# Chunked attention into a SoLU feed-forward: the attention's value products put directly behind the score products, and half of the attention's SBUF transfers issued by GpSimd

## Chip, core and metric

One NeuronCore of one Trainium2 chip. The metric is device microseconds of one execution, lower is better. Times are medians of several executions.

## What is computed

`q`, `k`, `v` are float32 of 8 batches x 8 heads x 576 tokens x 64. Attention runs inside chunks of 64 tokens; its output, 4608 tokens x 512, goes through a feed-forward with a softmax-gated unit and a layer norm. The reference, cut to that:

```
q_c, k_c, v_c = (t.reshape(B, H, nc, 64, D) for t in (q, k, v))
scores = matmul(q_c, k_c.T) / sqrt(D);  attn = softmax(scores)
x = matmul(attn, v_c)                       # -> (4608, 512)
h = x @ w_in                                # 512 -> 1024
solu = h * softmax(h)
ln = (solu - mean) / sqrt(var + 1e-06) * g_ln
out = ln @ w_out                            # 1024 -> 512
```

## The kernel before

The 4608 tokens are 36 tiles of 128 tokens (two chunks each). The large products are made in one-pass float32 form from high and low parts, so that each feed-forward product is three matmuls: `ffn_in` (tile `ph`, 24 matmuls of 128x512) takes `x_h`, `x_l` against `wi_h`, `wi_l`; `ffn_out` (tile `po`, 24 matmuls) takes `z_h`, `z_l` against `wo_h`, `wo_l`. The attention's two products are small: `scores` (`sx<-kT,qT`) and `values` (`sx<-attn_t,v_sb`), 8 matmuls of 64x128 each in the program, which the profile records as x16. Both write the one PSUM tile `sx` of two banks: bank 0 the scores, bank 1 the attention's output.

The first five tiles, the weights and the first loads are laid out by a hand-written list of words (`START`). From tile 5 on, one pass of the loop at the end works on several tiles at once. For tile i it: turns q and k of tile i+3 (`qk_turn`, VectorE transposes into `qT`, `kT`); turns `z` of tile i-1 (`z_turn`); splits `z` of the oldest queued tile into `z_h`, `z_l`; does `ffn_in(i)`, then `scores(i+3)`; starts `solu_a(i)`; and then runs three thirds of `ffn_out` of an older tile (`part()`, 8 matmuls each) with work between them: `softmax_a(i+3)`, `solu_b(i)`, `softmax_b(i+3)` and `values(i+1)` ahead of the second third, `attn_turn(i+3)` and `variance(i)` ahead of the last. `values` also copies its result out of PSUM as `x_h` (ScalarE) and `x_l` (VectorE). While `order.on` is set (from tile 5), TensorE, VectorE, ScalarE and GpSimd keep the order in which this is written. DMAs that are issued through `nc.sync` and `nc.gpsimd` are not held so: where they stand in their queues is left to the framework's scheduler.

Two operands change partitions by way of SBUF-to-SBUF DMAs, once for two tiles: VectorE transposes 32x32 blocks in place (`z` into `z_b`, `s_e` into `a_b`), and then 16 DMAs move the blocks of `z_b` to `z_t` (12 issued by SyncE, 4 by GpSimd), and 8 DMAs move those of `a_b` to `attn_t` (all issued by SyncE, L456). `attn_t` is a single buffer for a pair of tiles: `values` of the first tile of the pair waits for all 8 DMAs, and the next pair's DMAs wait for `values` of the second tile.

SyncE's queue (SP) also issues the loads: `q_st` and `k_st` (L293, 16 DMAs each for a batch, let out 14 to a tile) and `v_sb` (L352, one or two DMAs to a tile). GpSimd (POOL) does three vector operations per tile (`z<-z,nmean`, `s_e<-s_e,s_rinv`, `r<-u,mhalf`).

L42 is the helper through which the four ordered engines issue, so the profile shows most instructions at that line; they are told apart by tiles.

Of the kernel before, what the change touches and what calls it, by code (L numbers as in the profile page):

```python
# [27 lines left out]
class Order:  # L28
    """Engines whose instructions, while `on`, stay in the order they are written in."""

# [20 lines left out]
def chunk_attention_then_solu_ffn(  # L51
# [14 lines left out]
    P = 128  # L66
    CH = 64                      # tokens of an attention chunk
    NCH = S // CH                # chunks of a batch
    HP = H // 2                  # pairs of heads
    G = S // 32                  # groups of 32 tokens in a batch  # L70
    NT = B * S // P              # tiles of 128 tokens (two chunks)
    NCC = DM // P
# [46 lines left out]

    # ---- weights: to float32, then to high and low parts of 12 bits each (which is  # L120
    # exact), as products of one pass carry them. A piece is 128 rows of 512 columns.
    HALF = FF // 2
# [5 lines left out]
    def load_pair(x):  # L128
        """Two pieces by one load, in space that the tiles' loop takes over."""
        where, tag, bufs = (  # L130
            (work, "z_b", 1), (work, "z_t", 2), (stage, "q_st", 2), (stage, "k_st", 2)
        )[x if x < 2 else 2 + x % 2]
        raw = where.tile([P, 2, HALF, raw_words], U32, name="w_raw", tag=tag, bufs=bufs)
        src = (w_in, w_out)[x // NCC]
        m = x % NCC
        if x < NCC:
            dst, src = raw.rearrange("p x a b -> p (x a b)"), src[m * P:(m + 1) * P, :]
        else:
            dst = raw.rearrange("p x a b -> p x (a b)")
            src = src[2 * m * P:2 * (m + 1) * P, :].rearrange("(x p) n -> p x n", x=2)  # L140
        if x == 0:
            for n in range(2):
                cols = slice(n * HALF * raw_words, (n + 1) * HALF * raw_words)
                early[n:n] = [(dst[:, cols], src[:, cols])]
        else:
            nc.sync.dma_start(dst, src)
        for half in range(2):
            raws[pieces[2 * x + half]] = raw[:, half]
# [3 lines left out]
    def piece_scale(x):  # L152
        """The high words of a piece as float32 have the float64s' exponents in steps of 8;
        scaled by 2^-112 these have float32's bias (below float32's range they vanish,
        above it they are held at inf), and three bits to the left they are in place."""
        hi = raws[pieces[x]][:, :, 1]
        y = scaled[x] = work.tile(
            [P, HALF], F32, name="w_a", tag=("w_a", "o_sb")[x % 2]
        )
        act.activation(y, hi.bitcast(F32), AF.Abs, scale=2.0 ** -112)  # L160

    def piece_top(x):
        """A piece's float64s as sums of two float32: the high words' part, and the low
        words' with the same exponents. The high part of the weights is taken from the
        former."""
        kind, m, n = pieces[x]
# [52 lines left out]
    def piece_rest(x):  # L219
        """The sum of the two less the high part of the weights: their low part."""  # L220
        kind, m, n = pieces[x]
# [48 lines left out]

    # ---- attention operands: q as [(head of pair, d), pair, token]; k likewise by chunks,
    # with zeros where its head isn't the column's: [(head of pair, d), pair, chunk,
    # column's head of pair, key]; v as [(chunk, key), head, d]
    QT, V, QS, KS = {}, {}, {}, {}
    KT = [const.tile([P, HP, 2, 2, CH], F32, name=f"kT{x}") for x in range(2)]
    # the same for the attention, transposed: [(chunk, key), column's chunk, token / 32,
    # tile of pair, head, token % 32]
    AT = const.tile([P, 2, 2, 2, H, 32], F32, name="attn_t")
# [9 lines left out]
    def qk_loads(b):  # L288
        """The loads of a batch's q and k: [(head of pair, d / 32, token % 32), pair,
        token / 32, d % 32]."""  # L290
        def load(t, src, h, db):
            p0 = (h % 2) * D + db * 32
            nc.sync.dma_start(  # L293
                t[p0:p0 + 32, h // 2, :, :],
                src[b, h, :, db * 32:db * 32 + 32].rearrange("(g t) d -> t g d", t=32),
            )
        loads = []
        for src, dst, name in ((q, QS, "q_st"), (k, KS, "k_st")):
            t = stage.tile([P, HP, G, 32], F32, name=name)
            dst[b] = t  # L300
            loads += [
                (load, t, src, h, db) for h in range(H) for db in range(2)
            ]
        return loads
# [5 lines left out]
    def qk_turn(i):  # L310
        """A tile's q and k from their stage, transposed."""
        (b0, n0), (b1, n1) = chunk_of(i, 0), chunk_of(i, 1)
# [20 lines left out]
    def tile_parts(i):  # L333
        """A tile's parts of different batches: partitions, batch, first token."""
        (b0, n0), (b1, n1) = chunk_of(i, 0), chunk_of(i, 1)
        if b0 == b1:
            return [(0, P, b0, n0 * CH)]
        return [(0, CH, b0, n0 * CH), (CH, P, b1, n1 * CH)]

    def load_natural(i):  # L340
        """The first tiles' q and k, with tokens on partitions."""
        for x, src in enumerate((q, k)):
            for p0, p1, b, s in tile_parts(i):
                nc.sync.dma_start(
                    nat[p0:p1, i % 2, x],
                    src[b, :, s:s + p1 - p0, :].rearrange("h t d -> t h d"),
                )
# [28 lines left out]

    # ---- the stages of a tile of 128 tokens
    st = {}
    # a bank for the scores, one for the attention's output
    sx = ps_a.tile([P, 2, 512], F32, name="sx")  # L380
# [38 lines left out]
    def attn_transpose(i):  # L419
        """By the tensor engine, for the first tiles."""  # L420
        a = st.pop((i, "e"))
# [17 lines left out]

    # For the others 32 by 32 blocks are transposed in place, then the blocks change  # L440
    # quadrants, for two tiles at once
    def attn_turn(i):
# [8 lines left out]
        if i % 2 == 1:  # L451
            for c in range(2):
                for x in range(2):
                    for y in range(2):
                        to, of = c * CH + x * 32, c * CH + y * 32
                        nc.sync.dma_start(  # L456
                            AT[to:to + 32, c, y].rearrange("p s h t -> p (s h t)"),
                            ab[of:of + 32, x].rearrange("p s h t -> p (s h t)"),
                        )

    def values(i):
        for hp in range(HP):
            for j in range(2):
# [5 lines left out]
                    stop=True,  # L469
                )  # L470
        xv = sx[:, 1, :]
        xh = work.tile([P, NCC, P], F32R, name="x_h")
# [9 lines left out]
    def ffn_in(i):  # L482
        xh, xl = st[i, "x"]
        ph = st[i, "h"] = ps_h.tile([P, 2, HALF], F32, name="ph")
        # the first tile's by pieces of weights
        sums = [(n, cc) for n in range(2) for cc in range(NCC)]
# [21 lines left out]
    def solu_b(i):  # L508
# [10 lines left out]
        )  # L519
        # 1e-6 of the variance, in units of the unnormalised solu  # L520
        ssum = small.tile([P, 1], F32, name="ssum")
# [24 lines left out]

    # z with the feed-forward's features on partitions: 32 by 32 blocks are transposed in
    # place, then the blocks change quadrants, for two tiles at once
    turned = {}
# [34 lines left out]
    def z_transpose(i, f):  # L584
        """The same by the tensor engine, for the first and the last tiles."""
        z, _ = st[i, "n"]
# [9 lines left out]
    def ffn_out(i, part, parts):  # L596
        zh, zl = ZH, ZL
        # the last tile's by halves of the columns, of which one is stored ahead
        halves = 2 if i == NT - 1 else 1
# [32 lines left out]

    # ---- start: the first tiles by way of the tensor engine, weights behind them
    NAT = -(-S // P)             # tiles with the first batch's tokens

# [19 lines left out]

    # thirds of second products in the slots
    def direct(m):
# [17 lines left out]
    def third_ahead():  # L675
        """The same, with the halves of the next tile's operand where they find room."""
        m, p = queue.pop(0)
# [24 lines left out]
    for i in range(first, NT):  # L702
        order.on = i >= ORD
        # the loads of the batch after the one whose tiles come up
        if i + 3 < NT and next_batch < B and chunk_of(i + 3, 0)[0] == next_batch - 1:
# [9 lines left out]
        load_some(14)  # L715
        ffn_in(i)
        if i + 3 < NT:
            scores(i + 3)
        solu_a(i)

# [12 lines left out]
        if i + 1 < NT:  # L733
            values(i + 1)
        part()
# [38 lines left out]
```

## Time and profile before

| | |
|---|---|
| time, median of 3 executions | 543.99 us (543.41 to 545.03) |
| span of the profiled execution | 542.3 us |
| the median less that span | 1.7 us |
| mean granted TensorE clock | 0.994 |
| busy: PE / VectorE / ScalarE / GpSimd | 95% / 78% / 44% / 32% |
| matmuls per tile in the loop | 24 `ph`, 24 `po`, 16 + 16 recorded on `sx` |

The page does not give the profiled execution's own time apart from its span; the three timed executions lie 1.1 to 2.7 us above that span. A row of the timeline reads: start in us, duration in us, engine, line, operation, tile written <- tiles read, shape, how many; in brackets the idle time of the engine before it and what ended it. SPq and POOL rows with DMA_DIRECT2D are issues of DMAs: their duration is the issuing engine's time, and the landing of the data is told apart. Matmuls are pipelined: a 128x512 matmul is shown as 0.39 us long, but the next starts 0.23 us after it.

### The profile page before, as it was taken

The numbers are of one execution on the slowest core, as the hardware profiler recorded it, in microseconds if no ns is written. First come the engines' busy times: TensorE is split into PE (matmuls) and PEld (weight loads), VectorE is DVE, ScalarE is ACT, GpSimd is POOL, SyncE is SP. The second block draws the span as 40 slices with busy tenths as digits, with TensorE's granted clock in tenths as the row PEclk, the third lists the DMA queues.
The fourth block names the chain that finished last, engine by engine and source line by source line (L and its number), as shares of the span: only waits on it lengthen the run. The fifth ranks groups of instructions, "written<-read, shape, count | busy, mean of one in ns | idle before, by whom it ended". The sixth has DMA issues, their size and how long they took to land.

```text
span 542.3 us, 8909 instructions
## 1 busy us (share of the span) xinstructions
PE 515.1 (95%) x3038; PEld 403.0 (74%) x3038; DVE 425.4 (78%) x748; ACT 239.3 (44%) x386; POOL 174.7 (32%) x226
## 2 busy tenths in 40 slices
PE   2768899999999999999999999999999999999997
PEld 2445677777777777777777777777777777778886
DVE  4999998888888888888887888888878888875441
ACT  4848774544444333333333344433343343434342
POOL 6564742323232323232323232323132323232210
PEclk9998989999999999999999999999999999999999
DMA  8997794458663577657863776566753424142311
GB/s 237 348 230 154 120 156 77 113 126 161 136 147 98 126 148 147 144 130 140 147 148 103 144 160 138 138 136 148 147 134 79 121 75 123 53 107 78 102 45 59
DMA packets 206493, 72.18 MB, mean 133 GB/s; under 512 B 188592, under 2 KB 189232, under 8 KB 206064
## 3 DMA queue, kind: packets, MB, share of 16 engines
q1 hardware_dynamic: 198944, 57.85, 51.6%
q10 hardware_dynamic: 5328, 9.44, 4.9%
q0 software_dynamic: 2176, 4.33, 3.4%
q8 instruction: 24, 0.39, 0.3%
q14 instruction: 21, 0.17, 0.1%
HBM read 36.97 MB, written 9.44 MB: 86 GB/s over the span
## 4 chain that ended last, share of the span: by engine, by line
PE 80%; DVE 8%; SPq 7%; DMA 3%; ACT 1%; issue 1%; POOL 0%; DVEq 0%; POOLq 0%
PE po L42 36%; PE ph L42 31%; PE sx L42 11%; DVE w_a L42 4%; SPq L293 3%; SPq L456 2%; PE tp L42 2%; SPq L566 2%; DMA v_sb<-in_v_dram 1%; DMA w_raw<-in_moe_w_in_dram 1%; DVE w_p L42 1%; SPq L352 1%; DVE z L42 0%; ACT kT L42 0%; DVE s_sum L42 0%
## 5 line engine op out<-in xcount | busy, mean ns | idle before, releaser
L42 PE MATMUL po<-wo_l,z_h 128*128 128x512 f32 (+1 forms) x288 | 115.4, 401 | 0.0
L42 PE MATMUL po<-wo_h,z_l 128*128 128x512 f32 (+1 forms) x288 | 114.7, 398 | 0.0
L42 PE MATMUL ph<-wi_h,x_l 128*128 128x512 f32 x288 | 112.2, 390 | 2.5 <-DVE x_l L42 2.5
L42 POOL TENSOR_SCALAR z<-z,nmean 128x1024 f32<-128x1024 f32 x36 | 42.0, 1167 | 225.0 <-DVE ssum L42 204.0
L42 PE MATMUL ph<-wi_l,x_h 128*128 128x512 f32 x288 | 112.7, 391 | 0.3 <-ACT x_h L42 0.3
L42 PE MATMUL ph<-wi_h,x_h 128*128 128x512 f32 x288 | 112.1, 389 | 0.0
L42 PE MATMUL po<-wo_h,z_h 128*128 128x512 f32 (+1 forms) x288 | 111.7, 388 | 0.0
L42 ACT ACTIVATE z<-ph,h_nmax 128x1024 f32<-128x1024 f32 x36 | 40.3, 1119 | 140.6 <-DVE h_nmax L42 140.6
L42 DVE TENSOR_REDUCE h_nmax<-ph 128x1 f32<-128x1024 f32 x36 | 44.0, 1223 | 48.2 <-PE ph L42 48.2
L42 PEld LDWEIGHTS po<-wo_h,z_l 128*128 128x128 f32 x288 | 54.1, 188 | 15.7 <-issue 5.1
L42 PEld LDWEIGHTS ph<-wi_h,x_l 128*128 128x128 f32 x288 | 54.1, 188 | 14.3 <-DVE x_l L42 3.1
L42 PEld LDWEIGHTS po<-wo_l,z_h 128*128 128x128 f32 x288 | 54.1, 188 | 14.1 <-issue 5.1
L42 PEld LDWEIGHTS ph<-wi_l,x_h 128*128 128x128 f32 x288 | 54.1, 188 | 12.2 <-ACT x_h L42 0.7
L42 PEld LDWEIGHTS ph<-wi_h,x_h 128*128 128x128 f32 x288 | 54.1, 188 | 10.9
L42 PEld LDWEIGHTS po<-wo_h,z_h 128*128 128x128 f32 x288 | 54.2, 188 | 10.0
L566 POOL DMA_DIRECT2D z_t<-z_b x68 | 35.0, 520 | 45.4 <-DVE z_b L42 27.5
L42 DVE SCALAR_TENSOR_TENSOR z<-ph,z 128x1024 f32<-128x1024 f32 x36 | 44.1, 1224 | 6.2 <-ACT z L42 6.2
L42 ACT ACTIVATE sq<-z 128x1024 bf16<-128x1024 f32 x36 | 38.1, 1058 | 23.4 <-POOL z L42 23.4
L42 ACT ACTIVATE o_sb<-po,r 128x512 f32<-128x512 f32 (+1 forms) x36 | 24.6, 684 | 47.9 <-PE po L42 47.8
L42 DVE TENSOR_TENSOR z_l<-z_t,z_h 128x1024 fp32r<-128x1024 f32 (+1 forms) x35 | 39.6, 1131 | 6.8 <-ACT z_h L42 6.7
L42 ACT CAST z_h<-z_t 128x1024 fp32r<-128x1024 f32 (+1 forms) x35 | 35.0, 1001 | 22.0 <-ACT o_sb L42 7.4
L42 POOL TENSOR_TENSOR s_e<-s_e,s_rinv 128x512 f32<-128x512 f32 x36 | 37.8, 1049 | 20.7 <-DVE s_rinv L42 20.7
(91 smaller groups left out, 724.0 us busy)
## 6 DMA issues: line engine op xcount, KB each, us to landing
z_t<-z_b SPq DMA_DIRECT2D x192, 64.0 KB, 2.0
out_dram<-o_sb ACTq DMA_DIRECT2D x35, 256.0 KB, 2.7
v_sb<-in_v_dram SPq DMA_DIRECT2D x32, 256.0 KB, 3.5
q_st<-in_q_dram SPq DMA_DIRECT2D x112, 72.0 KB, 2.6
k_st<-in_k_dram SPq DMA_DIRECT2D x112, 72.0 KB, 3.3
attn_t<-a_b SPq DMA_DIRECT2D x120, 64.0 KB, 2.1
w_raw<-in_moe_w_out_dram SPq DMA_DIRECT2D x4, 1024.0 KB, 6.8
z_t<-z_b POOLq DMA_DIRECT2D x64, 64.0 KB, 2.8
```

Of the source, the lines that this page charges most:

```text
L42: ins = make(*args, **kwargs)
L293: nc.sync.dma_start(t[p0:p0 + 32, h // 2, :, :], src[b, h, :, db * 32:db * 32 + 32].rearrange("(g t) d -> t g d", t=32),)
L352: nc.sync.dma_start(V[i][p0:p1], v[b, :, s:s + p1 - p0, :].rearrange("h t d -> t h d"))
L456: nc.sync.dma_start(AT[to:to + 32, c, y].rearrange("p s h t -> p (s h t)"), ab[of:of + 32, x].rearrange("p s h t -> p (s h t)"),)
L566: (nc.gpsimd if x == y else nc.sync).dma_start(zt[x * 32:(x + 1) * 32, y, of].rearrange("p s a t -> p (s a t)"), zb[y * 32:(y + 1) * 32, x ...
```

## The change

Three edits. In the loop, `values(i + 1)` moves from ahead of the second third of `ffn_out` to directly behind `scores(i + 3)`, so that TensorE does both attention products in one stretch. The copies of its result out of PSUM, `x_h` and `x_l`, become a function of their own, `x_split`, and stay where they were. And of the 8 DMAs from `a_b` to `attn_t`, the four with x == y are issued by GpSimd. (Comments are taken out too, which shifts line numbers: what was L566 is L570.) The diff, cut to these:

```diff
                 for x in range(2):
                     for y in range(2):
                         to, of = c * CH + x * 32, c * CH + y * 32
-                        nc.sync.dma_start(
+                        (nc.gpsimd if x == y else nc.sync).dma_start(
                             AT[to:to + 32, c, y].rearrange("p s h t -> p (s h t)"),
                             ab[of:of + 32, x].rearrange("p s h t -> p (s h t)"),
                         )
...
     def values(i):
...
+        if not order.on:
+            x_split(i)
+
+    def x_split(i):
         xv = sx[:, 1, :]
...
         ffn_in(i)
+
         if i + 3 < NT:
             scores(i + 3)
+        if i + 1 < NT:
+            values(i + 1)
         solu_a(i)
...
         if i + 3 < NT:
             softmax_b(i + 3)
         if i + 1 < NT:
-            values(i + 1)
+            x_split(i + 1)
         part()
```

TensorE's order around one tile of the loop, before: the last matmul of `ffn_in`, the scores, a third of `ffn_out`, the values (a row without xN is one matmul).

```order
L42 MATMUL ph<-wi_h,x_l 128x512
L42 MATMUL sx<-kT_96,qT 64x128 x8
L42 MATMUL po<-wo_l,z_h 128x512
L42 MATMUL po<-wo_h,z_h 128x512
L42 MATMUL po<-wo_h,z_l 128x512
L42 MATMUL po<-wo_l,z_h 128x512
L42 MATMUL po<-wo_h,z_h 128x512
L42 MATMUL po<-wo_h,z_l 128x512
L42 MATMUL po<-wo_l,z_h 128x512
L42 MATMUL po<-wo_h,z_h 128x512
L42 MATMUL sx<-attn_t,v_sb 64x128 x8
L42 MATMUL po<-wo_h,z_l 128x512
```

The same place after the change:

```order
L42 MATMUL ph<-wi_h,x_h 128x512
L42 MATMUL ph<-wi_h,x_l 128x512
L42 MATMUL sx<-kT_96,qT 64x128 x8
L42 MATMUL sx<-attn_t,v_sb 64x128 x8
L42 MATMUL po<-wo_l,z_h 128x512
L42 MATMUL po<-wo_h,z_h 128x512
```

The values have moved ahead of eight `po` matmuls; this is so in each of the 28 tiles of the loop that have both products (i from 5 to 32).

SyncE's queue from one pair's transfers to `attn_t` to the next pair's, at a place where a batch's q and k are being loaded, before:

```order
L456 DMA attn_t<-a_b 32x512 x8
L293 DMA q_st<-in_q_dram 32x18x32 x14
L352 DMA v_sb<-in_v_dram 128x8x64
L293 DMA q_st<-in_q_dram 32x18x32 x2
L293 DMA k_st<-in_k_dram 32x18x32 x4
L566 DMA z_t<-z_b 32x512 x12
L293 DMA k_st<-in_k_dram 32x18x32 x4
L456 DMA attn_t<-a_b 32x512 x8
```

And after, the same stretch:

```order
L456 DMA attn_t<-a_b 32x512 x4
L293 DMA q_st<-in_q_dram 32x18x32 x14
L352 DMA v_sb<-in_v_dram 128x8x64
L293 DMA q_st<-in_q_dram 32x18x32 x2
L293 DMA k_st<-in_k_dram 32x18x32 x9
L570 DMA z_t<-z_b 32x512 x12
L293 DMA k_st<-in_k_dram 32x18x32 x3
L352 DMA v_sb<-in_v_dram 128x8x64
L456 DMA attn_t<-a_b 32x512 x4
```

Four `attn_t` issues have left the stretch, and the scheduler has put four more `k_st` and one more `v_sb` into it: 46 issues from the first `attn_t` of one pair to the first of the next, where 45 stood. This row pattern comes three times in the changed queue; before, two of the three held 45 issues and the first 42.

GpSimd's queue after the change, over two tiles:

```order
L42 TENSOR_TENSOR s_e<-s_e,s_rinv 128x512
L456 DMA attn_t<-a_b 32x512 x4
L42 TENSOR_TENSOR r<-u,mhalf 128x1
L42 TENSOR_SCALAR z<-z,nmean 128x1024
L42 TENSOR_TENSOR s_e<-s_e,s_rinv 128x512
L42 TENSOR_TENSOR r<-u,mhalf 128x1
L570 DMA z_t<-z_b 32x512 x4
```

The four new issues stand between `s_e` and `r` of every second tile; before, `r` followed `s_e` there. VectorE's and ScalarE's orders are the same before and after.

## The prediction

> **What bounds the kernel now.** First the page: how full TensorE is, and whether its clock was cut.
>
> ```profile
> span 542.3 us, 8909 instructions
> PE 515.1 (95%) x3038; PEld 403.0 (74%) x3038; DVE 425.4 (78%) x748; ACT 239.3 (44%) x386; POOL 174.7 (32%) x226
> core 0: 542.3 us, clock 0.994
> ```
>
> TensorE is busy 95% at full clock, and a busy TensorE may still lose time between groups, so next the chain of waits, over two tiles in the middle:
>
> ```profile
> 263.37 1.02 PE sx L42 x16
> ...
> 266.43 1.02 PE sx L42 x16
> ...
> 271.30 5.44 PE ph L42 x24
> 276.74 1.02 PE sx L42 x16
> ...
> 279.80 0.25 issue
> 280.05 1.09 PE sx L42 x16
> ...
> 290.46 1.02 PE sx L42 x16
> ```
>
> The chain is TensorE alone. A tile takes 276.74 - 263.37 = 13.37 us from scores to scores; the next takes 13.72, because its values started late. 24 `ph` in 5.44 us make 0.227 us per large matmul, so the 48 large ones take 10.88 us, and the two attention stretches cost (13.37 - 10.88)/2 = 1.24 us each. How much of that is work, and how much is going in and out? The timeline of one stretch, and of the one place in the start where values follow scores directly, with the time of a single small matmul:
>
> ```profile
> 303.45 0.39 PE L42 MATMUL ph<-wi_h,x_l 128*128 128x512 f32 x1
> 303.76 1.09 PE L42 MATMUL sx<-kT,qT 128*64 128x128 f32 x16
> 304.79 0.50 PE L42 MATMUL po<-wo_l,z_h 128*128 128x512 f32 x1
> 305.13 0.40 PE L42 MATMUL po<-wo_h,z_h 128*128 128x512 f32 x1
> ...
> 93.29 1.09 PE L42 MATMUL sx<-kT,qT 128*64 128x128 f32 x16
> 94.22 1.04 PE L42 MATMUL sx<-attn_t,v_sb 128*64 128x128 f32 x16
> L42 PE MATMUL sx<-attn_t,v_sb x464: 272/273/323, 132.6 to 506.4; 128*64 128x128 f32 x155
> ```
>
> Going in, the scores start 0.31 us after the last `ph` (0.227 is usual); going out, the first `po` holds the array 0.34 us instead of 0.227. In the start's place the values come 0.93 us after the scores began, with nothing lost between. The 1.04 us of those values less one matmul's 0.27 is 0.77 us for seven steps (the sixteen records run in pairs): 0.11 a step, 0.87 us for eight. So a stretch is 0.87 us of work and 1.24 - 0.87 = 0.37 us of going in and out.
>
> **Part 1: one stretch instead of two.** The second stretch loses its 0.37 us: 28 tiles x 0.37 = **10.4 us saved**. The lower bound of a tile's saving is 1.24 - 0.93 = 0.31 (8.7 us in all), if the values paid the start's 0.93.
>
> The values also stop waiting for what they waited for before. The view of the tile `sx` and one row of the timeline:
>
> ```profile
>   DVE s_e L42: 9.5, 26
> 387.73 1.09 PE L42 MATMUL sx<-attn_t,v_sb 128*64 128x128 f32 x16 [0.59 <-DMA attn_t<-a_b]
> ```
>
> Twice in the loop the values start late, for `attn_t` that has not landed: 0.35 us (13.72 - 13.37), with 0.25 of it in the chain, and here about 0.6. If these vanish they give **1.0 us**; whether they do is part 3.
>
> **Part 2: what VectorE pays.** The values' start is released by VectorE's `s_e`, which reads the other bank: waits go by the whole tile `sx`. With the values ahead of the softmax, its first step `s_nmax` will then wait for the values' end, not the scores'.
>
> ```profile
> 301.60 1.18 DVE L42 TENSOR_TENSOR z_l<-z_t,z_h 128x1024 fp32r<-128x1024 f32 x1
> 303.87 1.23 DVE L42 TENSOR_REDUCE h_nmax<-ph 128x1 f32<-128x1024 f32 x1 [1.09 <-PE ph L42]
> 305.01 0.68 DVE L42 TENSOR_REDUCE s_nmax<-sx 128x8 f32<-128x512 f32 x1
> 309.28 0.64 DVE L42 TENSOR_TENSOR x_l<-sx,x_h 128x512 fp32r<-128x512 f32 x1
> 310.62 0.71 DVE L42 STREAM_TRANSPOSE a_b<-s_e 128x512 f32<-128x512 f32 x1 [0.70 <-POOL s_e L42]
> ```
>
> Values would end at 303.76 + 0.93 + 1.04 = 305.73, so `s_nmax` and all behind it on VectorE slip by about 0.75 us. I cost this at nothing, and name the cover. `x_l` would end at 309.92 + 0.75 = 310.7; the next `ffn_in` starts 271.30 - 263.37 = 7.9 us after the scores, less the 0.37 saved, at 311.3, and needs `x_l` in its third matmul, at 311.8. VectorE then idles 1.1 us before `h_nmax`, for `ph`, in this tile (one with a batch boundary, more transposes than most); the slip of 0.75 and a tile shorter by 0.37 use up just that. Where it is gone, `h_nmax` starts later, under a `s_nmax` that waits anyway. On GpSimd, `r` stands behind four DMA issues of 0.5 us; it is used when its tile is stored, three tiles later.
>
> What is not free: `a_b` ends at 312.1 instead of 311.3 while the values that read it come sooner. New scores of the next tile: 303.76 + 13.0 = 316.8, values 317.7. From `a_b` to the values 5.6 us are left. Before, the next values came 3.06 us behind their scores (266.43 - 263.37), at 303.76 + 13.37 + 3.06 = 320.2, 8.9 us after `a_b`.
>
> **Part 3: whether `attn_t` lands in 5.6 us.** The rows of SyncE's queue at the ends of the three stretches of the order in which a batch is loaded, a row for each kind, and the landing times of `attn_t`, then of GpSimd's `z_t`:
>
> ```profile
> 111.38 4.96 SPq L456 DMA_DIRECT2D attn_t<-a_b  x8
> 137.52 5.50 SPq L456 DMA_DIRECT2D attn_t<-a_b  x8
> ...
> 297.99 4.99 SPq L456 DMA_DIRECT2D attn_t<-a_b  x8
> 311.41 0.44 SPq L352 DMA_DIRECT2D v_sb<-in_v_dram  x1
> 323.78 2.23 SPq L293 DMA_DIRECT2D k_st<-in_k_dram  x4
> 326.12 4.95 SPq L456 DMA_DIRECT2D attn_t<-a_b  x8
> ...
> 351.48 5.26 SPq L456 DMA_DIRECT2D attn_t<-a_b  x8
> 381.24 4.95 SPq L456 DMA_DIRECT2D attn_t<-a_b  x8
> DMA to landing us min/median/max: 1.9/2.1/4.4
> L566 POOL DMA_DIRECT2D z_t<-z_b x68: 496/497/715, 100.8 to 514.3; - x68
> DMA to landing us min/median/max: 1.7/2.7/4.2
> ```
>
> An issue costs SyncE about 0.62 us (4.95/8). In an ordinary pair its four last issues start 3 x 0.62 = 1.9 us after `a_b` and land 2.1 later: 4.0 us of the 5.6. GpSimd's four: 3 x 0.5 + 2.7 = 4.2, at worst 5.7. Both fit.
>
> In the loaded stretches SyncE is late by itself: 26.14, 28.13 and 29.76 us from pair to pair, where two tiles take 26.74. Before, 8 issues needed 7 x 0.62 + 2.1 = 6.4 of 8.9, so 2.5 us of lateness were free; the last was late by 3.0, and its values waited about 0.6. The rule holds there. After: the second and third swap four `attn_t` (0.62) for four `k_st` (2.23/4 = 0.56) and one `v_sb` (0.44): +0.2, 28.3 and 30.0. The first, 42 issues to 46, gets seven `k_st` and a `v_sb` for four `attn_t`: +1.9, 28.0. Two tiles now take 26.0, so SyncE is late by 2.0, 2.3 and 4.0, and only 5.6 - 4.0 = 1.6 us are free: waits of 0.4, 0.7 and 2.4. The 13.72 us tile shows a wait of 0.3 beyond the rule, which I add once: **3.8 us of new waits**. Bounds: none, if SyncE gains speed when half the transfers leave it; and with the third's pace (29.76/45 = 0.66 an issue) in all three, 46 x 0.66 - 26.0 - 1.6 = 2.8 each, 8.3.
>
> The Trainium skill, DMA: Bandwidth & Descriptors, section "Issuing engines are not separate DMA queues", says that issuing from more engines saves only the sequencer's time, "usually small relative to the DMA itself". By it SyncE's issues could not make the values late, and the sum would be the first rival's 532.6. Here the row decides: 0.62 us of issue against 2.1 of landing, and the issues of one queue add up.
>
> **The sum.** 542.3 - 10.4 - 1.0 + 3.8 = 534.7 us of span. The median of the runs lies 1.7 above the profiled span: **536.4 us**.
>
> **Rivals.**
> - *SyncE keeps up*: no new waits, 544.0 - 11.4 = 532.6. For it: each pair has four issues fewer. Against: at the three loaded places the scheduler filled the gap. 0.17.
> - *Waiting costs queue time*: the values of the first tile of a pair wait on eight semaphores, now right between small matmuls. If that eats these tiles' saving, 14 x 0.37 = 5.2: 541.6. Against: before, both tiles of a pair take 13.37. 0.05.
> - *SyncE late in more pairs*: the 8.3 us and 3 us in further pairs eat the gain, about 544. 0.08.
> - *GpSimd's half lands late, slower*. Its four issues stand beside VectorE's transposes, which follow `a_b`. Were they held until `z_b` is turned, 2.1 us of `qT`, `kT` and 1.25 of `z_b` (rows below) put the landing at 3.3 + 4.2 = 7.5 us, 1.9 past the 5.6, in 14 pairs: 26.6 us, 559.2. From a hold of 2.2 us it outweighs what the change saves (0.8 x 14 = 11). Against: GpSimd's `z_t` issues at 314.87 ran at 0.5 each beside VectorE's `z_l`. 0.09.
>
> ```profile
> 311.29 0.70 DVE L42 STREAM_TRANSPOSE qT<-q_st 128x512 f32<-128x512 f32 x1
> 311.92 1.38 DVE L42 STREAM_TRANSPOSE kT<-k_st 64x512 f32<-64x512 f32 x2
> 313.33 1.25 DVE L42 STREAM_TRANSPOSE z_b<-z 128x1024 f32<-128x1024 f32 x1
> 314.50 1.18 DVE L42 TENSOR_TENSOR z_l<-z_t,z_h 128x1024 fp32r<-128x1024 f32 x1
> 314.87 2.05 POOL L566 DMA_DIRECT2D z_t<-z_b  x4 [2.88 <-DMA q_st<-in_q_dram]
> ```
>
> The Trainium skill, SBUF — State Buffer, section "SBUF: two separate sides", states this hold for VectorE's two-port modes: GpSimd cannot write descriptors meanwhile, 620 ns becoming about 3100; by that figure four issues would take 12.4 us (an estimate), and the time would be far above 559. The `z_t` row shows none for `z_l`; no row shows GpSimd issuing beside a transpose.
>
> **How the numbers follow.** The forecast has 0.61. A measurement of this kernel can tell about 0.3%, 1.6 us, from no change. Faster: 0.61 + 0.17 + 0.05, **0.83**; same, the late-in-more-pairs case, **0.08**; slower **0.09**. The range leaves out only the slow rival and the worst of the waits: from no waits, 532.6 less 0.6 for the run's spread (543.41 against 543.99), **532.0**, to 8.3 us of waits, 540.9, and the semaphore rival's 541.6: **541.7**.
>
> **What would show it.** Right: TensorE's chain with one `sx` group of 32 per tile and 13.0 us from scores to scores in tiles without a wait; VectorE idle about 0.7 us before `s_nmax`, for TensorE's `sx`; the values waiting for `attn_t` from SyncE in about three loaded tiles, 3 to 4 us in all. Wrong: tiles at 13.37 (the stretch had no price of entry, or the semaphores took it); waits for GpSimd's DMAs in every pair; `ph` waiting for `x_l`.

## The result, and the profile after

| | before | after |
|---|---|---|
| median | 544.51 us (543.41 to 545.42, 4 executions) | 551.28 us (550.25 to 552.27, 4 executions) |
| span of the profiled execution | 542.3 us | 550.5 us |

The changed kernel takes 1.0118 of the time of before (95% interval 1.0096 to 1.0141): 1.2% slower, where 536.4 us was forecast and the range ended at 541.7.

The page first. The columns are as before.

```profile
span 550.5 us, 8913 instructions
PE 509.4 (93%) x3038; PEld 407.5 (74%) x3038; DVE 427.0 (78%) x748; ACT 235.6 (43%) x386; POOL 205.4 (37%) x286
```

TensorE is busy 5.7 us less than before, so one stretch does cost less than two; but the span is 8.2 us longer, so TensorE now stands idle some 14 us more. The chain of waits, over one tile near the end of the loop, where no batch is loaded any more:

```profile
408.16 1.90 PE sx L42 x32
...
421.16 1.90 PE sx L42 x32
```

One group of 32 on `sx`, and 421.16 - 408.16 = 13.00 us from scores to scores. Here the forecast's tile is exactly what came out. What TensorE waits for in the loop (110 to 530 us; total, times, longest):

```profile
PE sx L42 <- DMA attn_t<-a_b: 13.6, 10, 4.0
PE sx L42 <- DMA q_st<-in_q_dram: 0.6, 1, 0.6
```

Ten waits of 13.6 us in all, not three of 3.8. The busy time by stretch, for three tiles with a wait, from a tile's first `ph` to the next tile's (the columns after the length: busy time and count of PE, PEld, VectorE, ScalarE and GpSimd; granted clock; DMA share; GB/s):

```profile
247.94:262.11 14.17, 13.25 (x82) 10.67 (x81) 10.94 (x19) 5.20 (x8) 4.79 (x8) 1.00 0.90 167
329.06:344.64 15.58, 13.22 (x81) 10.67 (x80) 10.94 (x19) 5.20 (x8) 4.76 (x8) 1.00 0.65 132
383.77:402.57 18.80, 14.80 (x82) 11.84 (x81) 12.33 (x23) 5.20 (x8) 5.36 (x9) 0.91 0.55 118
```

The first is an ordinary pair (1.17 us over 13.00), the second and third are loaded stretches (2.58 and 5.80 over). In the third, TensorE is also busy 1.6 us longer for the same work, and its clock is 0.91; that is looked at in the last section. Over all tiles, the time above 13.00 adds up to 18.6 us: 13.6 and 0.6 of waits, 1.6 of slow clock, about 0.2 more at each wait (2.58 where the wait's row says 2.36), and some 0.5 left over. Of it 11.0 lies in the three loaded stretches (2.6, 2.6, 5.8) and 7.6 in the other tiles.

The balance of the spans: -10.4 for the stretch, -1.0 for the old waits, +18.6, and +0.9 because the loop began that much later: +8.1, against 550.5 - 542.3 = 8.2.

Now an ordinary pair (not one of the three loaded ones), from the end of `a_b` to the values, in the timeline (VectorE, ScalarE's queue, SyncE's queue, GpSimd, TensorE):

```profile
248.06 0.71 DVE L42 STREAM_TRANSPOSE a_b<-s_e 128x512 f32<-128x512 f32 x1 [0.70 <-POOL s_e L42]
248.86 0.34 ACTq L635 DMA_DIRECT2D out_dram<-o_sb  x1
249.12 3.29 SPq L456 DMA_DIRECT2D attn_t<-a_b  x4
249.33 2.01 POOL L456 DMA_DIRECT2D attn_t<-a_b  x4 [1.30 <-issue]
249.36 1.38 DVE L42 STREAM_TRANSPOSE kT<-k_st 64x512 f32<-64x512 f32 x2
255.48 1.09 PE L42 MATMUL sx<-attn_t,v_sb 128*64 128x128 f32 x16 [0.92 <-DMA attn_t<-a_b]
```

and the view of the tile `attn_t`, of this pair: SyncE's four issues (minimum, median and maximum in ns, first and last start) and the landing of all eight transfers:

```profile
L456 SPq DMA_DIRECT2D attn_t<-a_b x4: 513/589/1467, 249.1 to 251.8; - x4
DMA to landing us min/median/max: 3.5/4.5/4.8
```

`a_b` ends at 248.77. Forecast was a last issue 1.9 us later, at 250.7, landing by 252.8. The last issue of SyncE starts at 251.8, because SyncE came 0.35 us late and one of the four took 1.47 us, and no transfer lands in less than 3.5: nothing before 255.3, and the values start at 255.48. Beside them runs the output store of 256 KB that ScalarE issues 0.1 us after `a_b`. Over the whole kernel the same view gives:

```profile
L456 SPq DMA_DIRECT2D attn_t<-a_b x60: 507/588/1596, 112.3 to 496.5; - x60
L456 POOL DMA_DIRECT2D attn_t<-a_b x60: 496/496/581, 112.8 to 496.7; - x60
DMA to landing us min/median/max: 2.1/3.6/4.9
```

3.6 us where before showed 2.1, for both halves (SyncE's 3.7, GpSimd's 3.5), and in every pair the last transfer to land is one of SyncE's. The pair shown is among the worst. In the pair whose `a_b` ends at 222.34, SyncE starts 0.03 us later and its last issue is at 224.2, as forecast; the landing of its eight is

```profile
DMA to landing us min/median/max: 3.5/3.8/4.0
```

so that the last lands 5.75 us after `a_b`, and the values wait 0.5 us. And a loaded stretch, SyncE's queue at the third of them:

```profile
358.49 3.43 SPq L456 DMA_DIRECT2D attn_t<-a_b  x4
362.02 7.62 SPq L293 DMA_DIRECT2D q_st<-in_q_dram  x14
...
377.72 8.69 SPq L570 DMA_DIRECT2D z_t<-z_b  x12
...
389.71 2.74 SPq L456 DMA_DIRECT2D attn_t<-a_b  x4
```

GpSimd's four of this pair went out at 385.15, right behind `a_b`; SyncE's start at 389.71, 5.1 us after `a_b`, because the loads and the twelve `z_t` stand ahead of them. (In the other two loaded stretches they start 2.4 and 2.45 us after it. In four of the other pairs, too, SyncE is late, by 0.35 to 1.2 us.)

VectorE's group of `s_nmax`, the step that was to slip:

```profile
L42 DVE TENSOR_REDUCE s_nmax<-sx 128x8 f32<-128x512 f32 x36 | 24.8, 690 | 33.7 <-PE sx L42 33.7
```

It waits 33.7 us for `sx`, about 0.7 a tile and more where the values are late; `ph` waits for VectorE's `x_l` nowhere in the loop.

### The profile page after: what moved, and what is told of

It is laid out like the page before. It is cut to its first block, busy times and chain, and to the rows that moved or that the text cites. A ratio compares the mean times of both kernels' runs of the same rounds, so it can differ in the third digit from the quotient of the medians.

```text
span 550.5 us, 8913 instructions
## 1 busy us (share of the span) xinstructions
PE 509.4 (93%) x3038; PEld 407.5 (74%) x3038; DVE 427.0 (78%) x748; ACT 235.6 (43%) x386; POOL 205.4 (37%) x286
## 5 line engine op out<-in xcount | busy, mean ns | idle before, releaser
L42 PE MATMUL po<-wo_h,z_l 128*128 128x512 f32 (+1 forms) x288 | 112.1, 389 | 0.0
L570 POOL DMA_DIRECT2D z_t<-z_b x68 | 35.0, 520 | 45.3 <-DVE z_b L42 24.6
L42 PE MATMUL sx<-attn_t,v_sb 128*64 128x128 f32 x576 | 38.5, 275 | 14.2 <-DMA attn_t<-a_b 13.6
L42 DVE TENSOR_REDUCE s_nmax<-sx 128x8 f32<-128x512 f32 x36 | 24.8, 690 | 33.7 <-PE sx L42 33.7
L42 PEld LDWEIGHTS sx<-attn_t,v_sb 128*64 128x64 f32 x576 | 32.0, 137 | 19.4 <-issue 17.6
```

The source lines that it names most:

```text
L42: ins = make(*args, **kwargs)
L570: (nc.gpsimd if x == y else nc.sync).dma_start(zt[x * 32:(x + 1) * 32, y, of].rearrange("p s a t -> p (s a t)"), zb[y * 32:(y + 1) * 32, x ...
```

## Experiments

Four theories stood open. **Two queues**: eight transfers from two queues within 2 us, beside the store, take longer each. **SyncE's order**: loads ahead of `attn_t` make SyncE late. **False wait**: the slip of VectorE takes the 0.7 us that would have been enough. **GpSimd harms**: the half on GpSimd is the mistake itself. Each ratio is against runs of the kernel before on the same chip (medians 544.09, 543.51 and 544.15 in the three groups). They agree within 1 us with the 544.51 of the result, so times of different groups are compared directly below.

**e1: all eight transfers on SyncE again**, the values still moved.

```diff
-                        (nc.gpsimd if x == y else nc.sync).dma_start(
+                        nc.sync.dma_start(
```

> The changed kernel with all eight attn_t transfers back on SyncE; the values stay behind the scores. Theory (the eight transfers, close together and beside the output's store, land 3.5 to 3.7 us after their issue instead of 2.1, so GpSimd's half saves less than its issue time, but it does save): SyncE's eight need 7 x 0.62 + 2.1 = 6.4 us of the 5.6 there are, so the ordinary pairs wait about 1 us each, the three loaded ones 3 to 6; attn_t lands in 2.1 to 2.6 at the median; 550 to 556 us. Rival (GpSimd's queue is what made the transfers late): waits shrink and the time falls below 546.

573.62 us, 1.0535 (1.0508 to 1.0562). A pair's issues in the timeline of SyncE's queue, then the waits of TensorE, then the page's row of transfers (count, KB, median us to landing):

```profile
432.02 5.18 SPq L456 DMA_DIRECT2D attn_t<-a_b  x8
```

```profile
PE sx L42 <- DMA attn_t<-a_b: 27.8, 15, 4.0
```

```profile
attn_t<-a_b SPq DMA_DIRECT2D x120, 64.0 KB, 2.0
```

Landing is back at 2.0, so the longer landing does come with the second queue. But the last issue starts 4.6 us after the first in this pair, and the waits double. The half on GpSimd is worth 22 us here: *GpSimd harms* falls. The time is beyond the 550 to 556 expected: SyncE is also 1.1 to 1.9 us late in three further pairs, and behind five of the waits TensorE's clock falls (0.976 in the mean), which by the tiles' lengths costs some 9 us more.

**e2: the half on GpSimd alone**, values where they were before.

```diff
-                        nc.sync.dma_start(
+                        (nc.gpsimd if x == y else nc.sync).dma_start(
```

> The kernel before with half of the attn_t transfers issued by GpSimd and the values where they were. Theory (crowding by two queues at once): attn_t lands in 3.0 to 3.6 us at the median although the values have not moved; TensorE has 8.9 us, so nothing waits in ordinary pairs; 542.5 to 545 us. Rival (the transfers land late because everything behind the scores slipped by 0.75 us into the store and the loads): attn_t lands in 2.1 to 2.4. If GpSimd's queue harmed VectorE or the other transfers by itself, the time would be over 548.

545.17 us, 1.0012 (0.9997 to 1.0027): no difference. The view of `attn_t`, then TensorE's waits in the loop, all of them:

```profile
DMA to landing us min/median/max: 1.9/3.6/5.4
```

```profile
PE sx L42 <- issue: 0.4, 1, 0.4
```

The landing is as long as after the change, 3.6, and nobody waits for it, since 8.9 us are free there (one wait of 0.4 us is left, where SyncE is 3.0 us late). So the price was there, and only the move of the values made it due.

**e3: two PSUM tiles in place of `sx`**, so that `s_nmax` waits for the scores alone.

```diff
-    sx = ps_a.tile([P, 2, 512], F32, name="sx")
+    sx = ps_a.tile([P, 512], F32, name="sx")
+    ax = ps_a.tile([P, 512], F32, name="ax")
...
```

> The changed kernel with the PSUM tile sx made into two tiles of one bank, so that the softmax no longer waits for the values. Theory (the false wait puts a_b 0.75 us later, and each pair's values wait for what a_b's transfers bring): VectorE's 0.7 us of idle before s_nmax goes, the waits for attn_t fall from 18.6 us to 9 to 12, 541 to 545 us. Rival (landing alone is late, a_b's time does not matter, for instance since SyncE is late in any case): no change, 549 to 552.

555.78 us, 1.0208 (1.0166 to 1.025); 541 to 545 was expected. The group of `s_nmax` on the page, and the waits:

```profile
L42 DVE TENSOR_REDUCE s_nmax<-sx 128x8 f32<-128x512 f32 x36 | 24.5, 679 | 3.3 <-PE sx L42 3.3
```

```profile
PE ax L42 <- DMA attn_t<-a_b: 10.9, 6, 3.4
```

The slip is gone (33.7 us of waiting became 3.3), `a_b` comes 0.7 us sooner, and the ordinary pairs wait 0 to 0.6 us. Yet four tiles grow, to 2.1, 4.3, 3.9 and 5.2 us over 13.00. About 1.5 us of each of the last three is slow clock behind the wait (their mean clock is 0.90 to 0.91), where the changed kernel had one such tile: that takes back what the waits gave (13.6 us became 10.9). SyncE's lateness looks like a backlog: in the first of the four, the pair at 220, SyncE reaches its `attn_t` 1.0 us later than in the changed kernel, while `a_b` ends 1.9 us sooner, so that it is 3.0 us late where it was on time. Besides, the loop began 2.6 us later than after the change, because another start was scheduled. *False wait* is not the main cause, though it takes part in ordinary pairs.

**e7: the output store later**, issued by ScalarE behind the exponential of `solu_a`: 6.1 us after `a_b` in the trace, where it stood 0.1 us after it.

```diff
-            nc.scalar.dma_start(out[i * P:(i + 1) * P, cols], o[:, cols])
+            held.append((out[i * P:(i + 1) * P, cols], o[:, cols]))
...
         solu_a(i)
+            let_out()
...
```

> The changed kernel with each output tile's 256 KB store issued by ScalarE about 8 us later in the tile, behind the exponential of the feed-forward, away from the attn_t transfers. Theory (the store is half of the crowding): attn_t lands in about 2.5 to 3.0 us, waits fall by 0.5 to 1 us in 14 pairs, 540 to 546 us. Rival (the two queues alone crowd each other): landing stays at 3.5, 549 to 552.

548.81 us, 1.0075 (1.0047 to 1.0103): 2.5 us less than after the change. The view of `attn_t`, and the waits:

```profile
DMA to landing us min/median/max: 1.9/2.7/4.7
```

```profile
PE sx L42 <- DMA attn_t<-a_b: 9.8, 7, 2.8
```

The time is above the 540 to 546 expected. Landing falls from 3.6 to 2.7, and of the pairs in which SyncE is on time only one in the loop still waits for `attn_t` by more than 0.3 us (0.67). Five pairs with SyncE 1.1 to 3.0 us late wait 1.4 to 2.8 us, and behind two of them the clock falls. So moving the store takes away more than half of the longer landing, and this cures one of two causes.

**e4, e10, e8 and e9: the order of SyncE's and GpSimd's DMAs held as written, 8 loads to a tile** in place of 14, with the loads written behind `z_turn`: on the changed kernel (e4), with the late store too (e10), with two PSUM tiles too (e8), and on the kernel before (e9).

```diff
-    pe, dve, act, pool = (
-        order.engine(e) for e in (nc.tensor, nc.vector, nc.scalar, nc.gpsimd)
+    pe, dve, act, pool, sp = (
+        order.engine(e)
+        for e in (nc.tensor, nc.vector, nc.scalar, nc.gpsimd, nc.sync)
...
-        load_some(14)
+        load_some(8)
...
```

> The changed kernel with the loads spread evenly: eight q and k loads to a tile instead of fourteen, and SyncE's and GpSimd's DMAs held in the order they are written in, so that 34 issues instead of 46 stand between a loaded pair's transfers and the next. Theory (two causes of the waits: SyncE behind its queue in the loaded stretches, and slow landing in all pairs): the three large waits (2.6, 2.6 and 5.8 us) shrink to the ordinary 0.7 to 1.2, all waits from 18.6 to 8 to 11 us, 539 to 545 us. Rival (slow landing alone): no change, 549 to 552.

> The same spreading and ordering, and the output's store issued about 8 us later in the tile as well. Theory: neither cause is left, waits of 0 to 2 us in all, tiles of 13.0 us throughout, 532 to 536 us. Rival (a third cause, such as GpSimd's own 0.55 us of starting late and its landing): waits of over 6 us remain, 538 or more.

> All three: loads spread and ordered, the store late, and sx as two tiles, by which the scheduler also lays the start out anew (in the run with sx split alone the loop began 2.6 us later). Theory: as the previous kernel, no waits at all, but the start's 2.6 us: 534 to 538 us. Rival (the false wait on sx still costs something when the transfers are on time): below 532.

> The kernel before with the loads spread and SyncE's order held, nothing of the change. Theory: TensorE's chain has only 1.0 us of waits to lose, 542.5 to 544.5 us. Rival (an even load of SyncE is worth something by itself, for example through the landing of the loads): below 541.

| | us | ratio (95% interval) |
|---|---|---|
| e4 | 562.8 | 1.0357 (1.0315 to 1.0399) |
| e10 | 559.03 | 1.0278 (1.0247 to 1.0308) |
| e8 | 549.78 | 1.0095 (1.0061 to 1.0129) |
| e9 | 553.15 | 1.0159 (1.0128 to 1.019) |

All four miss what was expected. e4 and e10 are worse than the changed kernel, and e9 shows that the order harms the kernel before as well, by 1.6%. (e8, with two PSUM tiles, is 9.3 us faster than e10: with SyncE late in most pairs, the 0.7 us that the false wait takes seems to count.) SyncE's queue in e10 shows why:

```profile
155.97 7.50 SPq L42 DMA_DIRECT2D z_t<-z_b  x12
163.51 5.29 SPq L42 DMA_DIRECT2D k_st<-in_k_dram  x8
168.92 2.64 SPq L42 DMA_DIRECT2D attn_t<-a_b  x4
```

`z_t`, which waits for `z_b`, is only issued at 155.97, after 5 us in which SyncE issues nothing, and then the eight `k_st` stand between `z_t` and `attn_t`: these start some 3 us after `a_b`. Fewer loads per tile are no help when they are written behind a transfer that waits. The next edit moves them.

**e11 and e12: the same as e4, with the loads ahead of `z_t`**; e12 also has the late store. Against e4:

```diff
+        load_some(8)
...
         z_turn(i - 1)
...
-        load_some(8)
         ffn_in(i)
```

> The changed kernel with DMAs in written order, eight loads to a tile, and now the loads ahead of z_t in the order, so that only the twelve z_t stand between z_b and the attn_t transfers. (Held in order with the loads behind z_t, SyncE idled until z_b and then was 3 us late to attn_t.) Theory (SyncE's lateness makes the large waits, the store beside the transfers the small ones): the large waits are gone, the small ones of 0.2 to 1.2 us stay in up to 14 pairs, 6 to 11 us in all, 538 to 544 us. Rival (no order of SyncE's helps, since loads in flight slow the landing): 546 or more.

> The same with the store 8 us later in the tile. Theory: both causes are gone, waits of 0 to 2 us in all, tiles of 13.0 us, 532 to 536 us, which is what the merged stretch saves. Rival (a third cause, GpSimd's late start or the landing under loads): waits over 5 us, 538 or more.

e11: **537.49** us, 0.9876 (0.9849 to 0.9903), 13.8 less than the changed kernel. e12: **535.04** us, 0.9831 (0.9807 to 0.9856), faster than both kernels. The waits for transfers to `attn_t` in e11:

```profile
PE sx L42 <- DMA attn_t<-a_b: 0.9, 2, 0.7
```

The loads now fill the time in which SyncE idled, SyncE starts 0.06 us after `a_b` in every pair, and 13.6 us of waits for `attn_t` are 0.9. Expected was that 6 to 11 us of small waits would stay, for the store is where it was; they went as well, and the landing fell to 3.0 us in the median. So SyncE's place in time was a part of the small waits too. In e12 the waits for `attn_t` are gone; first its waits, then an ordinary pair like the one above, in the timeline:

```profile
PE sx L42 <- DMA q_st<-in_q_dram: 0.6, 1, 0.6
PE sx L42 <- issue: 0.2, 1, 0.2
```

```profile
242.37 0.71 DVE L42 STREAM_TRANSPOSE a_b<-s_e 128x512 f32<-128x512 f32 x1 [0.69 <-POOL s_e L42]
243.14 2.86 SPq L42 DMA_DIRECT2D attn_t<-a_b  x4
243.63 2.01 POOL L42 DMA_DIRECT2D attn_t<-a_b  x4 [1.30 <-issue]
248.72 1.04 PE L42 MATMUL sx<-attn_t,v_sb 128*64 128x128 f32 x16
249.22 0.34 ACTq L42 DMA_DIRECT2D out_dram<-o_sb  x1
```

The values start 248.72 - 243.08 = 5.64 us after `a_b`, without a wait: the 5.6 us of the prediction. The store goes out behind them. From the loop's second tile on, every tile with scores and values takes 13.00 us.

**e13 and e14: e12 with two PSUM tiles** (e13), **and with all eight transfers on SyncE** (e14, the edit of e1).

> The same with sx as two tiles, which also changes the start (2.6 us later in earlier runs). Theory: nothing waits, the false wait on sx no longer matters, 534 to 538 us. Rival (it still matters): below 532.

> The previous kernel with all eight attn_t transfers on SyncE. Theory (issue time is what GpSimd's half saves): SyncE's eight need 7 x 0.62 + 2.1 = 6.4 us where a_b is 0.75 us earlier than in the changed kernel, 6.35, so waits of 0.2 to 0.5 us in 14 pairs, 537 to 543 us. Rival (crowding makes two queues no faster than one): the same time as the previous kernel within 1.5 us.

e13: 537.24 us, 0.9868 (0.9847 to 0.989). From the loop's third on its tiles are 13.00 too, and its loop began 2.4 us later (113.80 against 111.40): with the transfers in time the false wait costs nothing, and the 2.2 us are the start's. e14: 547.91 us, 1.0068 (1.0042 to 1.0093), 10.7 more than e13, above the 537 to 543 expected; by the tiles about 8.6 of it lie in the loop's pairs and 2.4 in the start and the first tile. Its waits, and one pair on SyncE:

```profile
PE ax L42 <- issue: 3.4, 10, 0.5
PE ax L42 <- DMA attn_t<-a_b: 2.0, 2, 1.1
```

```profile
250.24 5.43 SPq L42 DMA_DIRECT2D attn_t<-a_b  x8
```

Landing is 2.0 here, but the eight issues take 5.43 us in this pair and near 5 us in the others, and nearly every pair's tile is 0.35 to 0.7 us over 13.00 (this one 1.1). With GpSimd's half each transfer lands later, and yet the last of the eight is there sooner: 4.8 us after `a_b` in most pairs of e13, 6.4 in most of e14.

## Why the prediction was wrong, point by point

- **Part 1, the stretch: right.** 0.37 us a tile; every tile without a wait takes 13.00, save two with values that start 0.1 to 0.2 us late.
- **Part 2, VectorE: right.** `s_nmax` waits about 0.7 us a tile for the values' end, `x_l` is never late, `r` behind GpSimd's issues delays nothing. e13 beside e12 shows the slip costs nothing where the transfers are in time. The budget of 5.6 us was right too (5.64 in e12).
- **Part 3, ordinary pairs: the step that failed.** "In an ordinary pair its four last issues start 3 x 0.62 = 1.9 us after `a_b` and land 2.1 later: 4.0 us of the 5.6 ... Both fit." The 2.1 was read where SyncE issued alone, at 0.62 us intervals. With two queues and the store beside them it is 3.6 in the median, 4.5 in the pair shown, and the values of the pair shown start 6.7 us after `a_b`; the pairs in which SyncE is on time need 4.9 to 6.2 us to the last landing, not 4.0. So little or nothing is left for a late SyncE, and it is 0.35 to 1.2 us late in four of these pairs, which the forecast left out; with a landing of 2.1 even these would have been in time (5.2 us at most). (GpSimd's half was also costed from `a_b`, though its issues start 0.55 us behind it.) Of these pairs (and other tiles) 7.6 us came, where none was forecast. e2 shows the landing without the move, e1 its return to 2.0 with one queue, e7 the store's part.
- **Part 3, loaded stretches: right in kind, mis-sized.** The lateness was forecast as 2.0, 2.3 and 4.0 us and is 2.4, 2.45 and 5.1. In the third, pair to pair is 389.71 - 358.49 = 31.2 us where 30.0 was forecast, with 0.95 of it in the four `attn_t` issues (3.43 us for 4 x 0.62 = 2.48). In the second, SyncE's four transfers took 3.3 to 4.2 us to land and not 2.1. The tiles lost 2.6, 2.6 and 5.8 where 0.4, 0.7, 2.4 and 0.3 were forecast. With the measured lateness and a landing of 2.1 the waits would have been 5.4 us; the longer landing adds some 3.3, and the slow clock behind the third wait 1.6, a term that the sum did not have. The upper bound of 8.3 held SyncE's pace open, but the landing fixed at 2.1 and the ordinary pairs at nothing: that is why the range failed.
- **The Trainium skill's rule** (DMA: Bandwidth & Descriptors, section "Issuing engines are not separate DMA queues") has two halves. That all issuers share the same DMA engines and interleave, this case agrees with: landing goes from 2.1 to 3.6 us with the second queue (e2). That the issue time saved is usually small does not hold here: e14 against e13 is 10.7 us. The prediction argued against the second half and took no account of the first.
- **Rivals.** *SyncE keeps up*: no. *Semaphores between small matmuls*: no; tiles with them are 13.00. *SyncE late in more pairs*: close; it is late in four more, but only the longer landing makes that count, and three further pairs wait 0.3 to 0.5 us with SyncE on time. *GpSimd's half lands late*: the sign and the place, waits in many pairs, but not the mechanism. GpSimd's 60 issues took 496 ns in the median and 581 at most, beside VectorE's transposes too (`kT` at 249.36 above): nothing held them, their transfers land as fast as SyncE's (3.5 against 3.7 us), and the hold that the Trainium skill states (SBUF — State Buffer, section "SBUF: two separate sides") does not appear for these transposes.

The trace of before had a warning of the longer landing. In the pair at 405.6 the landing of SyncE's first four transfers, then of its last four, is

```profile
DMA to landing us min/median/max: 2.0/2.5/2.7
DMA to landing us min/median/max: 2.0/2.0/2.3
```

The store goes out 1.2 us after `a_b` there, beside the first four. The median hid that, and the values waited for the last.

Shown by removal: SyncE's lateness (e11, -13.8 us), the store (e7 -2.5, e12 against e11 -2.5), and both together (e12). e4 against e11 shows that the place of the loads decides; held order and 8 loads for 14 were not tried apart from it. Left open: why the landing is still 2.6 to 2.7 us with the store out of the way (e7, e12) against 2.0 from one queue; crowding by the eight themselves is argued, not shown.

## What to carry to other kernels

Moving a consumer ahead shortens the time of every transfer that feeds it: work out the new time from producer to consumer, and then the landing *under the new concurrency*, with all that other engines issue in the same microseconds, not as the old trace shows it. On a queue that is near its limit, what stands between a producer and its transfer decides more than how many issues there are; put loads where the queue would wait anyway, ahead of the transfer that waits, and hold that order. A second issuing engine can pay even if each transfer lands later.

## What the runs showed of the hardware

A wait of 4 us costs more than 4 us. The longest one of the changed kernel in TensorE's timeline, and the granted clock by stretch (the columns as above):

```profile
394.39 1.10 PE L42 MATMUL sx<-attn_t,v_sb 128*64 128x128 f32 x16 [4.00 <-DMA attn_t<-a_b]
391.96:395.37 3.41, 0.98 (x16) 0.88 (x16) 0.95 (x1) 1.20 (x2) 0.00 (x0) 1.00 0.64 117
395.37:398.78 3.41, 3.41 (x11) 2.69 (x9) 3.15 (x8) 1.10 (x2) 0.32 (x1) 0.50 0.49 102
```

Behind the wait the clock is halved for 3.41 us, and then full again: 1.6 us more. The shorter wait of the second loaded stretch had no such end:

```profile
338.05 1.09 PE L42 MATMUL sx<-attn_t,v_sb 128*64 128x128 f32 x16 [2.36 <-DMA attn_t<-a_b]
333.93:337.34 3.41, 1.76 (x20) 1.12 (x18) 1.54 (x2) 1.21 (x2) 0.00 (x0) 1.00 1.07 199
337.34:340.76 3.42, 2.71 (x23) 2.31 (x24) 1.55 (x3) 0.13 (x1) 0.00 (x0) 1.00 0.39 72
```

But a still shorter one in e7 had:

```profile
226.22 1.64 PE L42 MATMUL sx<-attn_t,v_sb 128*64 128x128 f32 x13 [1.90 <-DMA attn_t<-a_b]
222.90:226.32 3.42, 1.52 (x20) 0.98 (x20) 2.96 (x3) 1.04 (x1) 0.00 (x0) 1.00 0.66 157
226.32:229.73 3.41, 3.41 (x20) 2.79 (x21) 2.03 (x4) 1.30 (x3) 0.00 (x0) 0.50 0.30 96
```

So the length alone does not decide, but where the wait lies. In every run the clock changes only at the edges of windows of 3.41 us that follow each other through the run. The wait of 1.90 us lies in one window; of the 2.36 us, 1.65 lie in one and 0.70 in the next. Over the loops of all runs, 18 waits were followed by half clock, and each has 1.85 us or more of waiting inside the one window ahead of it; no window with 1.81 us or less was followed by half clock. The Trainium skill, TensorE: Matmul & The Clock Gate, section "Part 1: The HAM clock gate", puts the fall to half rate behind an idle window of about 3.4 us. The length of the window agrees; that TensorE must be idle all through it does not, and here the measurement decides.

A GpSimd issue starts later behind its producer than one of SyncE: 0.55 us after the end of `a_b` (243.63 against 243.08 in e12), where SyncE needs 0.06.
